# Causal attention's diagonal blocks packed into shared score columns, with zero-padded copies of V

## The chip, the cores and the metric

The kernel runs on one core of a Trainium2 chip. The metric is the device time of one execution in microseconds (us): the median of two runs is 317.3 (317.27 and 317.34). A core has five instruction queues that matter here: PE (TensorE, matrix products; its weight loads are listed apart as PEld), DVE (VectorE), ACT (ScalarE), POOL (GpSimd) and SP (SyncE), which here only issues DMAs. Each works through its own instructions in order and waits on the others by semaphores.

## The reference

2,048 tokens of width 640 go through a layer norm; an attention branch and a gated branch read the result, and the input is added at the end. The attention works on four segments of 512 tokens, with 32 heads of 20 columns. Inside a segment it is a causal softmax; a memory matrix per head carries the sums of the segments before.

```python
for s in range(N):                                   # N = 4 segments, L = 512
    logits = jnp.einsum('bhqd,bhkd->bhqk', qs, ks) * scale + mask
    p = _softmax(logits, axis=-1)
    a_dot = jnp.einsum('bhqk,bhkd->bhqd', p, vs)
    pq = phi(qs)
    num = jnp.einsum('bhld,bhde->bhle', pq, M)
    den = jnp.einsum('bhld,bhd->bhl', pq, z)[..., None] + 1e-06
    o = g * (num / den) + (1.0 - g) * a_dot
    M = M + jnp.einsum('bhld,bhle->bhde', phi(ks), vs)
    z = z + jnp.einsum('bhld->bhd', phi(ks))
...
g = _silu(_B_ref(xn, B_w_gate, B_w_up, B_w_down))    # (sigmoid(x Wg) * (x Wu)) Wd
return x + s * g
```

The mask lets query q see key k only if k <= q. Of the 512x512 scores of a head and segment, a little over half count.

## The kernel before, in words

**Layout.** Heads are worked on in 8 groups of four per segment. `KT` and `QT` hold keys and queries transposed: for group g, head r of the four has 20 rows from partition 32r on, and three more rows that carry a bound on the scores. So a score product has 23 rows, and the four heads of a group stand in four row strips of the PE array (`tile_position=(32 * r, 0)`). `V` holds values with tokens on partitions, 21 columns a head, the last of them ones, so that the sum of the weights comes out beside the weighted values; two such buffers alternate between segments.

**Score units.** `Sps` is one accumulator of 128x4x512: keys of one block of 128 on partitions, four heads, 512 columns of queries. A unit (`pair_units`, `scores`) fills it once, ACT turns it into weights with one exponential (`exps`, line 558) and POOL sets the weights above the diagonal to zero in each diagonal block of 128x128 (line 560). Key block 0 needs all 512 queries, block 1 the last 384, block 2 the last 256, block 3 the last 128. For two groups that makes five units: 512; 384+128; 256+256 of both groups; 512; 384+128. A segment has 20 units, and the kernel 80. There is one `Sps`, so the next unit's scores wait for the exponential of the last; up to four tiles of weights (`pt`) are kept.

**Values.** `attend_T` (a visit) computes weighted values for one group, transposed: four column strips of the PE array, one a head, 32 columns of V each (`tile_position=(0, 32 * r)`), four key blocks in turn into one accumulator `ApsT`. It comes two to four units after the group's scores. DVE turns the result (line 582), POOL scales it (590, 591), DVE turns it back (594). The last group of the last segment is done by `attend` instead, with the weights as the stationary side and results in token order.

**The order.** Everything is written out by hand order: one slot per score unit. At the start of a slot stands a visit, if one is due, then the unit's scores, and then other work up to the slot's share. The dense products (gate `gp`, up `up`, down `yp`) are cut into single matmuls and fill what is free; the rest (projections `psq`, `psv`, the memory products `am` and `dm`, output products `sp`, DMAs on SP's queue, DVE steps) has due times in slots in the table `TIMES`. In a slot ahead of a visit, dense matmuls are written as four quarter-width ones (`ORDER["columns"]`, line 128), otherwise as one (line 124).

**Shared buffers.** `mn` is a staging tile used by the phi step (`phi_min`) and by the first two normalised tiles of the next segment (`ln_norm`); the other two have tiles of their own. At the start of the kernel `mn` also holds the zeros for the first warming matmuls. `cb`, `dmb` and `o6` have tiles of their own. Normalised tiles are spilled to DRAM by SP (line 270) and come back transposed (274).

Of the kernel before, what the change touches and what calls it, by code (L numbers as in the profile page):

```python
# [9 lines left out]
P = 128  # L10
D = 640
H = 32
DH = 20
E1 = DH + 1
# [29 lines left out]
def pair_units(g):  # L44
    return [[(g, 0, 0, 512, 0)],
            [(g, 1, 0, 384, 128), (g, 3, 384, 128, 384)],
            [(g, 2, 0, 256, 256), (g + 1, 2, 256, 256, 256)],
            [(g + 1, 0, 0, 512, 0)],
            [(g + 1, 1, 0, 384, 128), (g + 1, 3, 384, 128, 384)]]

def segment_units(n):
    units = []
    for g in range(0, NG, 2):
        units += pair_units(g)
    return units

TIMES = dict(
    turn=(0.03, 0.27, 1.29), turn_last=(0.0, 0.135, 0.43), attend=0.36, last=(0.36, 0.75), rest=350, dot6=0.43, load6=0.48,
    dot7=1.92, load7=1.95, add=(4.27, 4.52), out=(5.25, 5.95, 7.25, 8.35, 8.74, 9.06, 9.45, 11.05), update=-1.2,
    mem=(2.23, 4.32, 3.0, 6.98, 6.98, 2.45, 9.09, 10.79), mem_spill=11.56, mem_T=14.4, mem_T_last=12.63,  # L60
    k_tok=2.04, dot3=13.22, dot5=17.84, load5=18.1, add5=19.86, dot6_last=19.55, load6_last=19.6, stats0=(0.53, 0.9, 1.65, 3.6),
    stats=(-0.55, 0.13, 1.32, 3.57), norm=(5.26, 5.72, 6.03, 6.29), norm_T=7.22, ready=12.0,
    K=(9.69, 10.07, 10.49, 13.82, 14.29), Q=(11.32, 11.72, 12.29, 12.45, 13.52), K_eng='vaava', Q_eng='avvav',
    V=(10.33, 13.33, 14.43, 14.63, 17.05, 17.66, 19.78, 20.06), V_eng='avaavvav', k_spill0=14.77, k_lay0=15.15,
    q_spill0=14.1, q_lay0=16.79, q_spill1=15.26, k_spill1=16.93, q_abs=(13.53, 14.84), bound=14.78,
    bound_mm=15.9, bound_lay0=18.6, load_x=13.95, phi_k=((7.15, 7.62, 8.3), (12.77, 13.52, 13.77)),
    phi_q=((16.0, 16.6, 17.12), (18.3, 18.7, 19.18)),
# [8 lines left out]
def kernel(  # L76
# [71 lines left out]
    warm = stg.tile([P, 3 * L], BF, name="mn")  # L148
    nc.vector.memset(warm[:, 0:L], 0.0)
# [33 lines left out]
    V = [t[:, 0:VN].rearrange("p (j h e) -> p j h e", j=4, e=E1) for t in Vflat]  # L183

# [7 lines left out]
    def late_constants(after):  # L192
# [7 lines left out]
        ones_columns(1)  # L200
        nc.gpsimd.memset(obs[0][:], 0.0)
# [39 lines left out]
    def ln_norm(n, j, mv, rs):  # L241
        if n > 0 and j < 2:
            if j == 0:
                seg["xn"] = stg.tile([P, 3 * L], BF, name="mn")
# [745 lines left out]
```

## Time and profile before

| | us | share of the span |
|---|---|---|
| median of two runs | 317.3 | |
| the profiled execution | 317.5 | |
| its span, first to last instruction | 315.7 | |
| granted clock over the span | 1.000 | |
| exponentials, 80 of 1.878 | 150.2 | 48% |
| masks, 128 of 0.660 | 82.5 | 26% |
| first score unit starts on PE | 35.9 | |
| last score unit starts on PE | 297.4 | |
| last matmul ends, about | 312.0 | |

A row of the groups view names the line, the engine, the operation, what it writes from what, the shapes and the count; behind the bar stand the busy time of the group, the mean duration of one instruction in ns, and the time that its engine sat idle ahead of it, with what ended most of it. In the timeline each row is a merged run of like instructions: its start, its length, and what it is. Lengths of matmuls include the way through the array and overlap with the next one's; what a run takes from PE is the distance from its start to the next run's start.

### The profile page before, as it was taken

What the parts mean: (1) busy time and instruction counts of PE and PEld (TensorE: products, weight loads), DVE (VectorE), ACT (ScalarE), POOL (GpSimd) and SP (SyncE); (2) the same over time, 40 slices, a digit from 0 to 9 for tenths busy, and PEclk for the clock granted to TensorE, in tenths of its full rate; (3) what the DMA queues carried; (4) which work ended last, traced back from release to release, by engine and by line L of the source; (5) the groups of instructions that cost most, each with busy time, mean ns of one, the idle gap of its engine ahead of it and who ended that gap; (6) DMA issues with size and microseconds to landing.
All of it is one profiled execution on the core that took longest, in us unless ns stands there. A gap on an engine that the chain in (4) does not pass through costs nothing.

```text
span 315.7 us, 10227 instructions
## 1 busy us (share of the span) xinstructions
PE 307.1 (97%) x4297; PEld 167.5 (53%) x4327; DVE 224.9 (71%) x507; ACT 226.6 (72%) x228; POOL 133.5 (42%) x231
## 2 busy tenths in 40 slices
PE   7999999999999999999999999999999999999995
PEld 4544444665545444654665454545466655444673
DVE  5473455654868988878869989788787776644575
ACT  3724478778798776778897869679897775777730
POOL 2870035535262544435453364444444353525313
PEclk9999999999999999999999999999999999999999
DMA  7984886410742383504953365239524000280202
GB/s 242 375 329 148 282 227 175 127 45 2 209 149 66 101 140 118 129 24 148 263 171 110 115 106 144 67 110 211 175 78 131 19 23 26 79 148 25 86 21 85
DMA packets 55246, 41.27 MB, mean 131 GB/s; under 512 B 25952, under 2 KB 53824, under 8 KB 55200
## 3 DMA queue, kind: packets, MB, share of 16 engines
q1 hardware_dynamic: 52656, 35.87, 41.4%
q10 hardware_dynamic: 2544, 4.75, 4.1%
q8 instruction: 34, 0.56, 0.7%
q14 instruction: 12, 0.10, 0.1%
HBM read 19.98 MB, written 14.73 MB: 110 GB/s over the span
## 4 chain that ended last, share of the span: by engine, by line
PE 95%; DMA 1%; issue 1%; DVE 1%; ACT 1%; SPq 0%; ACTq 0%
PE up L124 11%; PE gp L124 10%; PE yp L124 10%; PE psq L124 10%; PE Sps L550 8%; PE gp L128 6%; PE yp L128 6%; PE up L128 6%; PE ApsT L574 6%; PE psv L124 5%; PE psq L128 4%; PE sp L124 3%; PE sp L128 3%; PE psv L128 2%; PE sp L534 2%; DMA xt<-in_A_x_dram 1%
## 5 line engine op out<-in xcount | busy, mean ns | idle before, releaser
L558 ACT ACTIVATE pt<-Sps 128x2048 bf16<-128x2048 f32 x80 | 150.2, 1878 | 40.6 <-PE Sps L550 39.6
L560 POOL TENSOR_SCALAR_AFFINE_SELECT pt<-pt 128x512 bf16<-128x512 bf16 x128 | 82.5, 660 | 156.6 <-ACT pt L558 153.8
L437 DVE SCALAR_TENSOR_TENSOR hT<-tg,up 128x512 bf16<-128x512 bf16 x48 | 32.6, 678 | 24.0 <-PE up L124 10.0
L124 PE MATMUL up<-xnT,Wu 128*128 128x512 bf16 x146 | 40.3, 380 | 1.4 <-issue 1.1
L124 PE MATMUL gp<-xnT,Wg 128*128 128x512 bf16 x146 | 38.9, 379 | 0.6 <-issue 0.5
L426 ACT ACTIVATE tg<-gp 128x512 bf16<-128x512 f32 x48 | 28.6, 595 | 14.4 <-PE gp L124 10.0
L124 PE MATMUL yp<-Wd,hT 128*128 128x320 bf16 x246 | 38.2, 300 | 0.0
L550 PE MATMUL Sps<-QT,KT 23*128 23x384 bf16 (+3 forms) x512 | 31.9, 301 | 0.1
L124 PEld LDWEIGHTS <-hT 128*128 128x128 bf16 x246 | 22.7, 98 | 11.3 <-issue 3.0
L454 DVE SCALAR_TENSOR_TENSOR aa<-t,yp 128x320 bf16<-128x320 bf16 x32 | 15.3, 478 | 13.9 <-ACT t L453 13.8
L582 DVE STREAM_TRANSPOSE tb<-ApsT 128x512 f32<-128x512 f32 x31 | 22.0, 711 | 4.1 <-PE ApsT L574 4.0
L128 PE MATMUL gp<-xnT,Wg 128*32 128x512 bf16 x352 | 24.4, 380 | 0.0
L574 PE MATMUL ApsT<-pt,V 128*32 128x512 bf16 (+2 forms) x496 | 23.5, 299 | 0.0
L124 PEld LDWEIGHTS <-Wu 128*128 128x128 bf16 x159 | 14.2, 98 | 17.4 <-issue 4.0
L124 PEld LDWEIGHTS <-Wg 128*128 128x128 bf16 x152 | 14.1, 98 | 15.8 <-issue 1.9
L128 PE MATMUL yp<-Wd,hT 128*32 128x320 bf16 x552 | 21.9, 300 | 0.0
L128 PE MATMUL up<-xnT,Wu 128*32 128x512 bf16 x324 | 21.7, 380 | 0.0
L550 PEld LDWEIGHTS <-KT 23*128 23x128 bf16 x512 | 9.2, 92 | 23.5 <-issue 23.4
L594 DVE STREAM_TRANSPOSE obT<-ob 128x256 f32<-128x256 f32 x31 | 13.5, 434 | 11.1 <-POOL ob L591 11.0
L591 POOL TENSOR_TENSOR ob<-tb,rb 128x320 bf16<-128x320 f32 x27 | 19.9, 735 | 2.2
L124 PE MATMUL psq<-xnT,Wq 128*128 128x512 bf16 x82 | 19.4, 379 | 0.2
L124 PE MATMUL psv<-Wv,xnT 128*128 128x320 bf16 x115 | 18.5, 300 | 0.4 <-ACT xnT L670 0.4
(124 smaller groups left out, 442.2 us busy)
## 6 DMA issues: line engine op xcount, KB each, us to landing
KT<-Kd SPq DMA_DIRECT2D x32, 80.0 KB
QT<-Qd SPq DMA_DIRECT2D x32, 80.0 KB
out_dram<-xt SPq DMA_DIRECT2D x14, 160.0 KB
Wg<-in_B_w_gate_dram ACTq DMA_DIRECT2D x1, 1920.0 KB
Wu<-in_B_w_up_dram ACTq DMA_DIRECT2D x1, 1920.0 KB
xt<-in_A_x_dram SPq DMA_DIRECT2D x3, 640.0 KB
Wd<-in_B_w_down_dram SPq DMA_DIRECT2D x1, 1920.0 KB
Od<-odot SPq DMA_DIRECT2D x3, 640.0 KB
```

Source lines behind the costliest of these rows:

```text
L124: nc.tensor.matmul(out_, lhsT=lhsT, rhs=rhs, start=start, stop=stop, skip_group_check=True)
L128: nc.tensor.matmul(out_[cols], lhsT=lhsT[:, cols], rhs=rhs, start=start, stop=stop, tile_position=(0, 32 * r), skip_group_check=True)
L426: nc.scalar.activation(tg[:], gp[:], ACT.Tanh, scale=0.5)
L437: nc.vector.scalar_tensor_tensor(out=h[:], in0=seg[n]["tg"][:], scalar=1.0, in1=up[:], op0=ALU.add, op1=ALU.mult)
L454: nc.vector.scalar_tensor_tensor(out=s["aa"][j][:, hs], in0=t2[:], scalar=1.0, in1=yp[:], op0=ALU.add, op1=ALU.mult)
L550: nc.tensor.matmul(Sps[:, r, c0:c0 + ncol], lhsT=KT[32 * r:32 * r + DH + 3, g, kb * P:(kb + 1) * P], rhs=QT[32 * r:32 * r + DH + 3, g, q0: ...
L558: nc.scalar.activation(pt[:, :, 0:ntot], Sps[:, :, 0:ntot], ACT.Exp, scale=SCALE)
L560: nc.gpsimd.affine_select(out=pt[:, :, c0:c0 + P], in_=pt[:, :, c0:c0 + P], compare_op=ALU.is_ge, fill=0.0, base=0, pattern=[[0, 4], [1, P ...
L574: nc.tensor.matmul(ps[32 * r:32 * r + 32, q0:L], lhsT=Vflat[n % 2][:, off:off + 32], rhs=t[:, r, c0:c0 + ncol], start=(i == 0), stop=(i == ...
L582: nc.vector.transpose(tb[:].rearrange("p h e -> p (h e)"), ps[:].rearrange("p (a t b) -> p a b t", t=32, b=2))
L591: eng.tensor_tensor(to, of, by, op=ALU.mult)
L594: nc.vector.transpose(s["obT", g // 4][:, g % 4, :].bitcast(F32), ob[:].rearrange("p a e b -> p (a e b)").bitcast(F32))
```

## The change

The units are cut anew (`segment_units`). The 128 keys of a diagonal block are taken in halves of 64. Early queries of a block see only its first half of keys, and two such products, from two key blocks, are put one above the other in the same 64 score columns: one on partitions 0 to 63, one on 64 to 127. A unit is of one of three kinds, all 512 columns wide:

- A, one per group: keys 0-63 with all queries on the low half of the partitions; on the high half, keys 64-127 with queries from 64 on, and, in the first 64 columns, keys 128-191 with queries 128-191.
- B, one per group: keys 128-255 with queries from 192 on (320 columns) and keys 256-383 with queries from 320 on (192 columns), on all partitions.
- C, one per four groups: 128 columns a group. In the first 64, keys 256-319 with queries 256-319 on the low half and keys 384-447 with queries 384-447 on the high half; in the other 64, keys 384-447 and keys 448-511 with queries from 448 on.

That makes 8 + 8 + 2 = 18 units and slots a segment, 72 in all. Products onto one half of the partitions have 64 weight columns (tiles of 32x64), B's have 128. A column block that holds two key blocks is read twice by the value products, each time with a copy of V in which the partitions of the other are zero: `Z` holds, for one half of the groups, key blocks 0 and 2 on partitions 0-63 and key blocks 1 and 3 on 64-127, with zeros elsewhere. It is cleared once, and refilled by two DMAs on SP's queue for each half segment. A visit has 8 pieces instead of 4. Each mask becomes one for each pattern (152 in all for 128). The last `attend` takes queries in blocks of 64.

Buffers: three `pt` and one `ptc` for four `pt`; `mn` holds three normalised tiles, and the fourth shares a tile (tag `sc`) with `cb`, `dmb` and `o6`; `o6` is cleared in the last segment instead of at the start; the warming zeros lie in `ktok`'s tile. The due times in `TIMES` are rewritten for 18 slots, most of them as 0.9 of the old.

```diff
+HALF = P // 2
+GH = NG // 2
 def segment_units(n):
     units = []
-    for g in range(0, NG, 2):
-        units += pair_units(g)
+    for h in range(2):
+        for i in range(GH):
+            units += [("A", GH * h + i), ("B", GH * h + i)]
+            if i == 0:
+                units.append(("C", h))
     return units
...
+    ZW = H // 2 * E1
+    Zflat = cpool.tile([P, 4 * ZW + 32 - E1], BF, name="Z")
+    Z = Zflat[:, 0:4 * ZW].rearrange("p (a b w) -> p a b w", a=2, b=2)
+
+    def fill_Z(n, h):
+        src = Vflat[n % 2][0:HALF, 0:VN].rearrange("p (a b k w) -> p a b k w", a=2, b=2, k=2)
+        for b in range(2):
+            nc.sync.dma_start(Z[HALF * b:HALF * b + HALF, :, b, :], src[:, :, b, h, :])
...
+        nc.gpsimd.memset(Zflat[:], 0.0)
...
     def ln_norm(n, j, mv, rs):
-        if n > 0 and j < 2:
-            if j == 0:
-                seg["xn"] = stg.tile([P, 3 * L], BF, name="mn")
+        if j == 0:
+            seg["xn"] = stg.tile([P, 3 * D], BF, name="mn")
+        if j < 3:
             xn = seg["xn"][:, j * D:(j + 1) * D]
         else:
-            xn = lnp.tile([P, D], BF, name="xn", bufs=2)[:]
+            xn = stg.tile([P, D], BF, name="xn", tag="sc")[:]
...
+    def products(pieces):
+        for out_, keys, g, q0, q1 in pieces:
+            m, p0 = keys.stop - keys.start, out_[0]
+            for r in range(4):
+                rows = slice(32 * r, 32 * r + DH + 3)
+                nc.tensor.matmul(Sps[p0:p0 + m, r, out_[1]:out_[1] + q1 - q0], lhsT=KT[rows, g, keys],
+                                 rhs=QT[rows, g, q0:q1], start=True, stop=True, tile_position=(32 * r, p0))
+
     def scores(unit):
...
+        kind, g = unit
+        k = slice
+        if kind == "A":
+            products([((0, 0), k(0, 64), g, 0, L), ((HALF, 64), k(64, 128), g, 64, L),
+                      ((HALF, 0), k(128, 192), g, 128, 192)])
+        elif kind == "B":
+            products([((0, 0), k(128, 256), g, 192, L), ((0, 320), k(256, 384), g, 320, L)])
+        else:
+            for i in range(GH):
+                c, e = P * i, GH * g + i
+                products([((0, c), k(256, 320), e, 256, 320), ((HALF, c), k(384, 448), e, 384, 448),
+                          ((0, c + 64), k(384, 448), e, 448, L), ((HALF, c + 64), k(448, L), e, 448, L)])
 
     def exps(unit):
...
+        pt = ptp.tile([P, 4, L], BF, name="ptc" if kind == "C" else "pt", bufs=1 if kind == "C" else 3)
+        nc.scalar.activation(pt[:], Sps[:], ACT.Exp, scale=SCALE)
...
+        if kind == "A":
+            mask(low, lambda t: t[:, :, 0:64], [[0, 4], [1, 64]], 0)
+            mask(high, lambda t: t[:, :, 0:P].rearrange("p r (b c) -> p r b c", b=2), [[0, 4], [0, 2], [1, 64]], 0)
+        elif kind == "B":
+            for c0 in (0, 320):
+                mask(slice(0, P), lambda t: t[:, :, c0:c0 + 64], [[0, 4], [1, 64]], 64)
+        else:
+            mask(low, lambda t: t.rearrange("p r (i b c) -> p (r i) b c", b=2, c=64)[:, :, 0, :],
+                 [[0, 4 * GH], [1, 64]], 0)
+            for i in (0, GH // 2):
+                cols = slice(P * i, P * i + P * GH // 2)
+                mask(high, lambda t: t[:, :, cols].rearrange("p r (b c) -> p r b c", c=64),
+                     [[0, 4], [0, GH], [1, 64]], 0)
...
+    def pieces(n, g, which):
...
+        out = [(a, 0, 64, 64, L), (a, "Z0", 0, 0, 64), (a, "Z1", 0, 128, 192),
+               (b, 1, 0, 192, L), (b, 2, 320, 320, L),
+               (c, "Z2", i, 256, 320), (c, "Z3", i, 384, 448), (c, 3, i + 64, 448, L)]
...
-    def attend(n, todo):
+    def attend(n, which):
...
+        for values, v, t, c0, q0, q1 in pieces(n, NG - 1, which):
             for r in range(4):
...
+                for q in range(q0, q1, HALF):
+                    p0 = q % P
+                    nc.tensor.matmul(acc["ps"][p0:p0 + HALF, q // P, r, :],
+                                     lhsT=t[:, r, c0 + q - q0:c0 + q - q0 + HALF], rhs=src[:, off:off + E1],
+                                     start=p0 not in acc["begun"], stop=True, tile_position=(0, p0),
+                                     skip_group_check=True)
...
+    fill_Z(0, 0)
     load_x(1)
...
-    SLOTS, SEG = len(units), 20
+    SLOTS, SEG = len(units), 4 * GH + 2
...
+    for n in range(NSEG):
+        for g in range(NG if n < NSEG - 1 else NG - 1):
+            visits[unit_of[n, "B", g] + (3 if g % GH == 0 else 2)] = (n, g)
...
+        for h in range(2):
+            if n or h:
+                at(t0 + TIMES["fill"][h], 0, fill_Z, n, h)
```

## The prediction

> **What bounds the kernel now.** I read the engine totals and the slices of the page first, then the chain, then the costliest groups, and then single stretches of TensorE's timeline, because the totals leave only one engine to look at.
>
> ```profile
> PE 307.1 (97%) x4297; PEld 167.5 (53%) x4327; DVE 224.9 (71%) x507; ACT 226.6 (72%) x228; POOL 133.5 (42%) x231
> ...
> PE   7999999999999999999999999999999999999995
> ...
> PEclk9999999999999999999999999999999999999999
> ...
> PE 95%; DMA 1%; issue 1%; DVE 1%; ACT 1%; SPq 0%; ACTq 0%
> ...
> L558 ACT ACTIVATE pt<-Sps 128x2048 bf16<-128x2048 f32 x80 | 150.2, 1878 | 40.6 <-PE Sps L550 39.6
> L560 POOL TENSOR_SCALAR_AFFINE_SELECT pt<-pt 128x512 bf16<-128x512 bf16 x128 | 82.5, 660 | 156.6 <-ACT pt L558 153.8
> ```
>
> PE is busy in nine tenths or more of every slice but the first and the last, at a full granted clock, and is 95% of the chain. The exponentials wait for PE (39.6 us), not PE for them. So shorter ACT work moves nothing; the time changes by what changes on PE. Busy is not price, so I price PE by the distance from one start to the next:
>
> ```profile
> 45.70 0.59 PE L124 MATMUL gp<-xnT,Wg 128*128 128x512 bf16 x2
> 46.23 0.39 PE L550 MATMUL Sps<-QT,KT 23*128 23x512 bf16 x4
> 46.56 0.83 PE L128 MATMUL gp<-xnT,Wg 128*32 128x512 bf16 x12
> 47.21 1.25 PE L128 MATMUL up<-xnT,Wu 128*32 128x512 bf16 x20
> 48.29 1.25 PE L128 MATMUL gp<-xnT,Wg 128*32 128x512 bf16 x20
> 49.37 0.72 PE L574 MATMUL ApsT<-pt,V 128*32 128x512 bf16 x16
> 50.02 0.40 PE L550 MATMUL Sps<-QT,KT 23*128 23x384 bf16 x8
> 50.35 1.25 PE L124 MATMUL up<-xnT,Wu 128*128 128x512 bf16 x4
> ...
> 98.25 0.81 PE L390 MATMUL dm<-V,ktok 128*32 128x63 bf16 x80
> 98.87 0.41 PE L128 MATMUL gp<-xnT,Wg 128*32 128x512 bf16 x4
> ...
> 298.38 0.75 PE L610 MATMUL Aps<-V,pt 128*128 128x21 bf16 x24
> ...
> 298.99 3.15 PE L124 MATMUL yp<-Wd,hT 128*128 128x320 bf16 x22
> ```
>
> Four things are read here. Twenty quarter-width matmuls of 512 columns take 1.08 us (47.21 to 48.29): four column tiles run together, 216 ns for 512 columns, 0.42 ns a column. Four row tiles of a score unit also run together (46.23 to 46.56), but 0.33 us is 0.11 more than 0.216: that is the change of tile shape. The same extra stands ahead of it (0.53 for two matmuls of 216). Eighty matmuls of 63 columns take 0.62 us, 7.8 ns each: singly, a round of four starts 28 to 30 ns after the last for the first 28, and then the matmuls come 8.3 ns apart. Full-width matmuls of 21 columns come 25 ns apart (0.61 over 24).
>
> **The change, part by part.** All PE terms are in us for the whole kernel; the code gives the counts, these rows the prices.
>
> *Changes of tile shape.* In program order the kernel before alters the shape 163 times, the changed one 151 times: 16 fewer around 8 fewer score units, 4 more around the two last attends, now in 128x64 tiles. At 0.105 each: -1.26. The new shapes' own changes aren't in the trace; the four kinds that are lie between 0.10 and 0.11.
>
> *Score streams.* Before, each of 32 groups streams 512, 384, 128 and 256 columns on four row tiles: 216 + 173 + 53 + 109 = 551 ns start to start, 17.6 in all. Now a group has A: 512 columns on one column half, 448+64 on the other. If the halves run together as the row tiles and the column tiles do, A takes the 216 of its longer half plus some 15 for the staggered starts: 231. B: 320+192 by the row of 384+128 (173 for the first): 226. C, per four groups, is 64 matmuls of 64 columns over eight tiles. Its lower end is 8 rounds of 29 = 232 ns, its upper end 64 matmuls at 8 ns = 512 (also the 16 rounds that half overlap would make). The nearest row, the 80 short ones, starts 28 at the pace of the tiles and then goes by 8.3: 28 x 29/8 + 36 x 8.3 = 400, which I take. Sum: 32 x 0.457 + 8 x 0.40 = 17.8, so +0.2 (from -1.1 to +1.1).
>
> *Values.* 31 visits of 32 matmuls for 16, over the same 1,280 columns: five short rounds at 29 to 32 ns where 27 would be the share of the columns, and four more matmul rounds at 2 to 3 ns. +11 ns a visit, +0.35 (0 to +0.75).
>
> *Last attends.* 80 matmuls of 21 columns for 40. If the two halves overlap, 12.5 ns each, the price stays at 1.0; if not, 25 each, +1.0. I take 0, since column tiles overlap in every row that has them.
>
> *Wide or narrow dense matmuls.* More of them stand in slots before a visit, so 2,288 quarter-width ones instead of 1,888; at 1.08 for twenty against 1.08 to 1.09 for five: 0.
>
> *ACT, POOL, DVE.* Eight exponentials fewer: 8 x 1.878 = 15.0 off ACT, none of it on the path. POOL's 128 masks become 152 over as many elements; 128x128 takes 290 ns and 128x512 takes 660, so 0.96 ns an element, and the 20-row mask of Ind (160 elements, 475) adds about 8 ns a row. A has 0.41+0.69, B 2 x 0.41, C 3 x 1.25. That is some +7 on 133.5 of 315.7: nothing, as long as C is in time (a rival). The clearing of Z is about 1.25 (840 elements take 0.80) in POOL's idle time from 22.6 to 38.3. The clearing of o6 (0.55) moves from 1.7 to the last segment: nothing.
>
> *Z copies.* Sixteen issues of 0.4 on SP's queue. The first pair stands between QT's bounds (done 31.87) and x, Wd, the second spill, the token-order K and the second relayouts: 0.8 later each. Wd is first read at 54.03, after 20 us of cover; without cover, 0.8 once. Later pairs follow oT's load and hold up its last part and the token-order K by 0.8: in the trace the load is issued at 109.24, the next spill at 110.26, and the reader of Z comes four slots after 102.60, about 117. The waits on Z's last reader are for a visit that is already past. Cost 0.
>
> *xn in mn.* The third normalised tile now shares mn with the phi step, whose minimum waits for that tile's spill. In the trace the spills are issued from 124.63, the minimum starts at 127.50 and the transpose, which needs both spills landed, at 127.62. So DVE might wait 0 to 0.3, three times, with the queued evacuations and turns behind it; PE has four rotating accumulators ahead of it. I take 0, at most +0.9. At the start xn loses one wait of 0.5 on a transpose, on DVE alone: 0.
>
> Sum: -1.26 + 0.2 + 0.35 + 0 = -0.7. The profiled execution took 317.5 (its span 315.7 and 1.8 around it), which makes 316.8; the median of the two runs is 317.3, so I forecast **316.6**. With the lower ends: -1.26 - 1.1 = -2.4, 314.9. With the upper ends: -1.26 + 1.1 + 0.75 + 1.0 = +1.6, 318.9.
>
> **Rivals.** *The column halves do not overlap (slower).* No row has row tiles and column tiles at once. Then A streams 216 + 189 + 29 = 434 instead of 231, 32 x 0.203 = +6.5, and C takes 512 instead of 400, +0.9. Together 316.6 + 7.4 = **324.0**. It passes 2% (6.3 us) only if nearly all of the overlap, 7.0 of 7.4, is lost. For it: each direction alone leaves the other whole. Against: four column tiles read all 128 rows at once without loss (47.21), twice the streams that the halves need. Chance 0.12. The Trainium skill (TensorE: Matmul & The Clock Gate, "Measured speedup vs the span model") reports that row and column tiles compose, nine tiles at 6.32 times one; no run here shows it yet, and it speaks for the forecast.
>
> *Loading 64 columns of weights sets the pace.* The trace has loads of 128 columns at full width within 25 ns (298.38) and of 32 in quarter tiles within 29 ns. If a load in column tiles goes by its columns, 64 take 58: C becomes 8 x 58 = 464 (+0.5), and 40 units that open with such a load are 29 later each (+1.2): 316.6 + 1.7 = **318.3**. For it: PE changes shape first and loads then. Against: the extra after a change is the same 0.10 to 0.11 for 32 and 128 columns. Chance 0.12. The Trainium skill says that column tiling rules out fast weight loads (TensorEngine Tiling (Array Packing), "Feature Incompatibilities") and puts a load at the columns over 1.2 ns (TensorE: Matmul & The Clock Gate, "LDWEIGHTS"), 53 ns for 64; with that C would be 427 and the sum 0.2 higher, and our 25 ns for full-width pairs is a faster load than that rule's 107.
>
> *C's masks come late.* The visit is two slots after C, and 73 slots over some 266 us are 3.65 each: about 6.8 us from C's scores to the visit. Exponential and its wait 2.1, three masks 3.75: 5.85. It decides from 1.57 us a mask on, and each 0.1 above costs 8 x 0.3 = 2.4; at 1.86 it is over 2%, at a price by rows of 165 ns (660 over 4) it would be **342**. Against it: 20 rows cost 475 in all. Chance 0.04.
>
> *Over 2% faster* would need 6.3 off PE; all that eight score units cost is 8 x 0.43 = 3.4. Chance 0.02. That fewer units are not made is excluded: 72 exponentials stand in the changed program.
>
> **How the numbers follow.** The forecast has 0.70. The range takes its own ends and the second rival's (318.3, and 1.2 for its unknowns), 314.7 to 319.5, and leaves out the first and third rivals and the faster case, 0.18. A measurement of this kernel tells 2% from no change. Faster 0.02; slower the third rival and somewhat over half of the first, 0.11; same the rest, 0.87.
>
> **What would show it.** Right: A's second four matmuls start within 0.02 us of the first four and the next work 0.34 after A's start; C's next work 0.34 to 0.6 after its start; a visit 0.66; 72 exponentials, ACT near 212, PE still at 97%. Wrong: A at 0.54 (first rival), a C unit near 0.6 with wider gaps ahead of every 64-column load (second), PE idle ahead of the first visit of each half (third), or a new idle on PE behind a DVE wait for Xd.

## The result

The changed kernel took 328.34 us (median of 2 runs, 328.19 to 328.48) beside 317.3 for the kernel before: a ratio of 1.0348, interval 1.0303 to 1.0392. The prediction was 316.6, in a range of 314.7 to 319.5, and none of its rivals' times (324.0, 318.3, 342) is near. The profiled execution took 328.48, its span 326.8, so 11.1 of span have to be found. The page of the changed kernel, in the rows that were read before:

```profile
PE 311.0 (95%) x5743; PEld 180.5 (55%) x5776; DVE 230.3 (70%) x507; ACT 213.6 (65%) x220; POOL 146.4 (45%) x256
...
PE   6999999999999999999998998899999999999995
...
PEclk9999999999999999999999999999999999999999
...
PE 72%; DMA 7%; DVE 7%; ACT 5%; SPq 4%; issue 3%; POOL 2%; ACTq 0%; DVEq 0%
...
L624 ACT ACTIVATE pt<-Sps 128x2048 bf16<-128x2048 f32 x64 | 120.0, 1875 | 39.1 <-PE Sps L602 34.8
L627 POOL TENSOR_SCALAR_AFFINE_SELECT pt<-pt 128x256 bf16<-128x256 bf16 (+2 forms) x128 | 64.9, 518 | 138.4 <-ACT pt L624 132.8
...
L627 POOL TENSOR_SCALAR_AFFINE_SELECT ptc<-ptc 64x1024 bf16<-64x1024 bf16 x24 | 28.3, 1195 | 16.1 <-ACT ptc L624 15.5
```

ACT's total is as forecast (213.6 for 212), and so is each C mask (1.2); POOL has 13 more where some 7 were forecast. The clock is full. What changed is the chain: PE had 95% of it and now has 72%; DVE, ACT, DMA and SP's queue have come in. PE's slices show 8s in the second half, where there had been only 9s. PE's timeline tells whether its own work is as priced:

```profile
48.89 0.42 PE L602 MATMUL Sps<-QT,KT 23*64 23x512 bf16 x12
49.25 1.05 PE L166 MATMUL up<-xnT,Wu 128*32 128x512 bf16 x16
...
52.49 0.36 PE L673 MATMUL ApsT<-pt,V 128*32 128x448 bf16 x4
...
53.16 0.40 PE L602 MATMUL Sps<-QT,KT 23*128 23x320 bf16 x8
...
79.29 0.71 PE L602 MATMUL Sps<-QT,KT 23*64 23x64 bf16 x64
79.93 0.39 PE L162 MATMUL gp<-xnT,Wg 128*128 128x512 bf16 x1
...
308.17 0.58 PE L710 MATMUL Aps<-V,pt 128*64 128x21 bf16 x25
...
309.21 2.08 PE L162 MATMUL yp<-Wd,hT 128*128 128x320 bf16 x14
```

A lasts 0.36 from its start to the next work, a visit 0.67: both as forecast, so the column halves overlap (in the trace's single records the second half's four matmuls start 13 ns behind the first four). C lasts 0.64 in place of 0.505 (0.40 and the change of shape). The first of the last attends takes 1.04 for 48 matmuls of 21 columns: 19.5 ns each, not 12.5.

To split the 11.1, I priced every matmul of each program, in its order, by the prediction's distances from start to start, with C and the last attends at what they measured. The real distance from the first scores to the last matmul, less that sum, is time in which PE waited, with whatever the prices have wrong. Before: 275.8 measured, 275.1 priced, 0.7 of waits. Changed: 285.4 measured, 275.9 priced, **9.5 of waits**. So PE's work costs 0.8 more (it should have been 0.7 less), the waits 8.8 more, and the first scores start at 37.33 in place of 35.87, 1.5 more: together 11.1. The largest waits behind the first scores, from the view of waits, with their sum, how many, and the longest:

```profile
PE sp L166 <- ACT tg L473: 1.5, 1, 1.5
PE psv L162 <- DVE aa L501: 1.4, 1, 1.4
PE Sps L602 <- ACT pt L624: 1.4, 3, 0.6
```

They are short and far apart, some behind ACT's work and some behind DVE's. The first of them in the timeline of the changed kernel (engines mixed, in order of time):

```profile
200.77 0.92 DVE L412 TENSOR_SCALAR mn<-ktok 128x1280 bf16<-128x1280 bf16 x1
...
201.72 1.27 ACT L417 ACTIVATE mn<-mn 128x1280 bf16<-128x1280 bf16 x1 [2.43 <-DVE mn L412]
...
202.90 1.86 ACT L624 ACTIVATE pt<-Sps 128x2048 bf16<-128x2048 f32 x1
...
203.14 0.61 PE L166 MATMUL gp<-xnT,Wg 128*32 128x512 bf16 x8
...
204.65 0.59 ACT L473 ACTIVATE tg<-gp 128x512 bf16<-128x512 f32 x1
...
205.29 0.46 PE L166 MATMUL sp<-Wo,oT 128*32 128x320 bf16 x8 [1.55 <-ACT tg L473]
```

ACT does its work in program order. Phi's exponential (L417) stands ahead of the exponential of the scores and waits 2.43 for its minimum, which DVE reaches only after the memory parts. The scores' exponential and the tanh of the gate behind it are late by as much, the gate's accumulator is not free, and PE waits 1.55 for one. In the kernel before, phi's exponential was due at 7.62, behind slot 7's exponential. Most due times from slot 2 on were scaled by 18 to 16 slots (2 + 5.62 x 8/9), not plainly by 0.9, which makes 6.996 of it: just ahead of slot 7's.

That gave theory O: the waits come from which steps share a slot and in which order they queue, since scaled due times fall otherwise on the grid of 18 slots. (The first four expectations still word it more narrowly, as slots with too little work between two score units.) Its first rivals were S (the staging buffers that are now shared) and Q (the Z copies on SP's queue).

### The profile page after: what moved, and what is told of

The parts are those of the page before. It is cut to its first block, busy times and chain, and to the rows that moved or that the text cites. A ratio compares the mean times of both kernels' runs of the same rounds, so it can differ in the third digit from the quotient of the medians.

```text
span 326.8 us, 13190 instructions
## 1 busy us (share of the span) xinstructions
PE 311.0 (95%) x5743; PEld 180.5 (55%) x5776; DVE 230.3 (70%) x507; ACT 213.6 (65%) x220; POOL 146.4 (45%) x256
## 4 chain that ended last, share of the span: by engine, by line
PE 72%; DMA 7%; DVE 7%; ACT 5%; SPq 4%; issue 3%; POOL 2%; ACTq 0%; DVEq 0%
PE psq L162 8%; PE up L162 7%; PE gp L162 7%; PE gp L166 7%; PE Sps L602 7%; PE up L166 6%; PE yp L162 6%; PE psq L166 4%; ACT pt L624 4%; PE ApsT L673 4%; PE yp L166 4%; PE psv L162 4%; PE sp L162 2%; SPq L514 2%; DMA xnT<-Xd 2%
## 5 line engine op out<-in xcount | busy, mean ns | idle before, releaser
L624 ACT ACTIVATE pt<-Sps 128x2048 bf16<-128x2048 f32 x64 | 120.0, 1875 | 39.1 <-PE Sps L602 34.8
L627 POOL TENSOR_SCALAR_AFFINE_SELECT pt<-pt 128x256 bf16<-128x256 bf16 (+2 forms) x128 | 64.9, 518 | 138.4 <-ACT pt L624 132.8
L627 POOL TENSOR_SCALAR_AFFINE_SELECT ptc<-ptc 64x1024 bf16<-64x1024 bf16 x24 | 28.3, 1195 | 16.1 <-ACT ptc L624 15.5
L602 PE MATMUL Sps<-QT,KT 23*64 23x64 bf16 (+4 forms) x1152 | 31.9, 257 | 1.4 <-ACT pt L624 1.4
L162 PE MATMUL yp<-Wd,hT 128*128 128x320 bf16 x197 | 30.9, 300 | 0.0
L166 PE MATMUL up<-xnT,Wu 128*32 128x512 bf16 x424 | 29.3, 380 | 0.0
L166 PEld LDWEIGHTS <-hT 128*32 128x32 bf16 x748 | 19.5, 97 | 7.0 <-issue 1.8
L602 PEld LDWEIGHTS <-KT 23*64 23x64 bf16 (+1 forms) x1152 | 13.8, 100 | 17.1 <-issue 14.4
L673 PE MATMUL ApsT<-pt,V 128*32 128x448 bf16 (+2 forms) x372 | 20.8, 300 | 0.4 <-DVE aa L545 0.4
L500 ACT ACTIVATE t<-yp 128x320 bf16<-128x320 f32 x32 | 13.8, 434 | 9.9 <-PE yp L162 6.8
```

Source lines behind the costliest of these rows:

```text
L162: nc.tensor.matmul(out_, lhsT=lhsT, rhs=rhs, start=start, stop=stop, skip_group_check=True)
L166: nc.tensor.matmul(out_[cols], lhsT=lhsT[:, cols], rhs=rhs, start=start, stop=stop, tile_position=(0, 32 * r), skip_group_check=True)
L500: nc.scalar.activation(t2[:], yp[:], ACT.Tanh, scale=0.25)
L602: nc.tensor.matmul(Sps[p0:p0 + m, r, out_[1]:out_[1] + q1 - q0], lhsT=KT[rows, g, keys], rhs=QT[rows, g, q0:q1], start=True, stop=True, ti ...
L624: nc.scalar.activation(pt[:], Sps[:], ACT.Exp, scale=SCALE)
L627: nc.gpsimd.affine_select(out=blocks(pt[rows]), in_=blocks(pt[rows]), compare_op=ALU.is_ge, fill=0.0, base=base, pattern=pattern, channel_ ...
```

## The experiments

"Waits" is worked out as above, on the profiled execution (the 8.5 of the expectations counts only those over 0.15 us). The ratios are those on record, which need not be the quotient of two medians. Times are in us.

| kernel | median (range, runs) | ratio to before, interval | waits |
|---|---|---|---|
| before | 317.3 to 317.8 by batch | | 0.7 |
| changed | 328.34 (328.2 to 328.5, 2) | 1.0348, 1.0303 to 1.0392 | 9.5 |
| a_own | 329.16 (327.9 to 331.5, 4) | 1.0374, 1.0322 to 1.0427 | 10.0 |
| a_nofill | 328.61 (328.2 to 329.7, 4) | 1.0354, 1.0330 to 1.0378 | 9.5 |
| b_share | 317.37 (317.1 to 318.1, 10) | 0.9998, 0.9988 to 1.0007 | |
| b_fill | 317.73 (317.2 to 318.2, 10) | 0.9999, 0.9985 to 1.0013 | |
| r_k | 331.59 (328.5 to 332.7, 4) | 1.0416, 1.0359 to 1.0472 | 12.4 |
| r_phi | 327.65 (327.0 to 328.4, 4) | 1.0308, 1.0279 to 1.0337 | 8.7 |
| b_k | 320.30 (319.3 to 322.0, 6) | 1.0088, 1.0059 to 1.0116 | 2.7 |
| b_phi | 324.26 (323.0 to 324.9, 4) | 1.0196, 1.0164 to 1.0227 | 5.8 |
| r_slots | 325.92 (324.6 to 327.1, 4) | 1.0266, 1.0224 to 1.0308 | 6.5 |
| c_wide | 328.95 (1) | | 13.4 |
| r_mix | 325.49 (324.5 to 326.1, 4) | 1.0241, 1.0217 to 1.0266 | 6.9 |
| r_mix_st | 325.00 (324.4 to 326.5, 4) | 1.0243, 1.0209 to 1.0278 | 7.0 |
| r_20 | 324.11 (321.7 to 326.5, 4) | 1.0198, 1.0125 to 1.0270 | 3.2 |
| b_early | 320.99 (320.7 to 321.3, 4) | 1.0099, 1.0081 to 1.0117 | 4.6 |
| b_late | 330.39 (330.2 to 331.3, 4) | 1.0405, 1.0380 to 1.0430 | 12.4 |
| r_20_cw | 320.50 (320.0 to 324.0, 5) | 1.0086, 1.0070 to 1.0103 | 7.9 |
| r_20_st | 323.10 (321.5 to 324.2, 4) | 1.0171, 1.0136 to 1.0206 | 4.6 |
| r_20_z | 323.17 (322.0 to 325.5, 6) | 1.0174, 1.0136 to 1.0212 | 4.0 |

### Is it the shared buffers or the Z copies?

a_own gives the third normalised tile a buffer of its own again; a_nofill leaves out all Z copies but the first pair, so later segments use the first one's values there. b_share puts the changed kernel's shared staging into the kernel before; b_fill adds 16 copies of V to the kernel before, on SP's queue at the same places (to a scratch tensor).

```
a_own     seg["xn"] = stg.tile([P, 3 * L], ...); j == 2: xn = stg.tile([P, D], BF, name="xn2")
a_nofill  for h in range(2): at(t0 + TIMES["fill"][h], ...)   removed
b_share   xn: mn (j < 3) or tag "sc"; cb, dmb: tag "sc"; mn = [P, 3 * D]; warm in ktok
b_fill    at(t0 + (1.5, 11.6)[h], 0, fill_Z, n, h)            added
```

> The changed kernel with a tile of its own for the third normalised tile; mn is as small as before. Theory S (shared staging): the phi step's minimum waits for the third tile's spill, ACT's queue stands behind its exponential, and PE runs into full accumulators; in the changed trace the stalls of PE at 130 to 135 and 199 to 205 us (about 3.5 us) are of this kind, so 324 to 326. Theory Q (Z copies make SP's queue late) and theory O (fewer, longer slots leave too little work between two score units): no change, 328.3.

> The changed kernel with only the first pair of Z copies; the 14 later DMAs are left out, so later segments read old copies of V. Theory Q: the Q spill and the second half of the phi step on Q come 1 to 3 us sooner, the stalls at 156 and 173 us (about 1.9) go, 325.5 to 326.5. Theories S and O: 328.3, at most 0.5 less.

> The kernel before with the changed kernel's staging buffers alone: three normalised tiles in mn, the fourth in one tile with cb, dmb and o6, the warming zeros in ktok's tile. Theory S: 3 to 5 us slower, 320 to 322. Theories Q and O: 317.3, within 0.5.

> The kernel before with the changed kernel's 16 copies of V on SP's queue at the same due times by its longer segment, into a scratch in DRAM that nothing reads. Theory Q: 1.5 to 3 us slower, 319 to 320. Theories S and O: 317.3, within 0.5.

Neither. Each taken away leaves the changed kernel where it was, and the largest wait, 1.55 for the gate's tanh, stays (at 205.29 in the changed kernel, 204.71 in a_own, 205.40 in a_nofill). Each added to the kernel before costs nothing, to within 0.15%. S and Q fall; the prediction's zeros for them stand.

### Single due times, in both kernels

r_k and r_phi undo one move each in the changed kernel; b_k and b_phi make the same two moves in the kernel before.

```
r_k    K[4]     12.924 -> 13.02
r_phi  phi_k[0] (6.578, 6.996, 7.6) -> (6.578, 7.3, 7.8)
b_k    K[4]     14.29 -> 13.95
b_phi  phi_k[0] (7.15, 7.62, 8.3) -> (6.578, 6.996, 7.6); mem[3], mem[4] 6.98 -> 6.427; out[2] 7.25 -> 6.667
```

> The changed kernel with one due time altered: the fifth K item of a segment moves from slot 12 (12.924) to slot 13 (13.02), as it stood before the change, where the fourth and the fifth K fell in two slots. Theory O (the due times, scaled by 0.9, fall otherwise on the grid of 18 slots, and PE waits where a slot is too short or a queue is in the wrong order): slots 13 and 49, which held two V pieces alone (1.8 us of PE work against an exponential of 1.88 and its hand-overs), grow to 2.9; the waits of PE at 90.7 and 229.0 us (0.66 each) and at 165.1 (0.22) go, 1.5 us in all, so 326.8 (325.5 to 327.3, more if the 1.5 us at 173 goes with them). Theory P (PE's own work is dearer than priced, the waits are only where slack shows): the same 328.3. Theory M (the waits move on to the next slot, since DVE and ACT are behind in any order): 327.9 to 328.6, with new waits of the same sum within three slots.

> The changed kernel with two due times altered: the exponential of the first phi step on ktok moves from 6.996 to 7.3, its end from 7.6 to 7.8, so that ACT does it after slot 7's exponential, as before the change, and not ahead of it. Theory O: ACT no longer stands 2.4 us at phi's minimum ahead of the exponential of the scores, the waits at 199.4 and 205.3 us (0.71 and 1.72) and at 130 to 135 (1.1) shrink to under 0.5 in all: 325.3 (324.8 to 326.5). Theory P: 328.3. Theory M: the minimum is as late as before and the wait shows up behind the next ACT or DVE work: 327.5 to 328.6.

> The kernel before, with the fifth K item moved from slot 14 (14.29) into slot 13 (13.95): slot 13 then holds two K, one Q and one V item (4.9 us of PE work), and slot 14 two V pieces alone (1.8), in each of the three segments, the pattern of the changed kernel. PE's work is the same. Theory O: one to three waits of 0.2 to 0.7 behind the short slots, as in the changed kernel: 318.6 (317.9 to 319.5). Theories P and M: within 0.4 of 317.4.

> The kernel before, with the last memory parts of the first half, the first phi step on ktok and the third output item given the slot times of the changed kernel (6.427, 6.427; 6.578, 6.996, 7.6; 6.667): phi's exponential then stands ahead of slot 7's on ACT. PE's work is the same. Theory O: ACT waits for phi's minimum ahead of the exponential of the scores, once in each of the segments 1 and 2, and PE waits 1 to 2.4 us each time: 320.3 (318.9 to 322). Theories P and M: within 0.5 of 317.4.

The kernel before answers as theory O says, and more strongly: b_k costs 2.5 and b_phi 6.5, both beyond the ranges expected. b_k, in its timeline, where the slot was left with two V pieces:

```profile
85.03 0.40 PE L550 MATMUL Sps<-QT,KT 23*128 23x384 bf16 x8
...
85.36 1.53 PE L124 MATMUL psv<-Wv,xnT 128*128 128x320 bf16 x10
85.54 1.88 ACT L558 ACTIVATE pt<-Sps 128x2048 bf16<-128x2048 f32 x1 [0.35 <-PE Sps L550]
...
87.47 0.40 PE L550 MATMUL Sps<-QT,KT 23*128 23x512 bf16 x4 [0.58 <-ACT pt L558]
```

PE has 1.8 us of work between two score units, the exponential between them ends 2.4 after the first unit's start, and the one score tile is not free: 0.64 lost, at 87.5, 154.5 and 220.6, once in each of the first three segments. b_phi, in the same view:

```profile
197.22 1.27 ACT L370 ACTIVATE mn<-mn 128x1280 bf16<-128x1280 bf16 x1 [2.10 <-DVE mn L365]
...
198.40 1.86 ACT L558 ACTIVATE pt<-Sps 128x2048 bf16<-128x2048 f32 x1
...
200.31 0.40 PE L550 MATMUL Sps<-QT,KT 23*128 23x512 bf16 x4 [2.12 <-ACT pt L558]
```

This is the start of the changed kernel's chain, phi's exponential ahead of that of the scores, made in the kernel before by due times alone. In the changed kernel the other way is only half open. r_phi takes the wait of 1.55 and the 0.45 at 135 away and gives 0.7 (forecast: 3). r_k takes away the waits behind two of the three short slots, as expected (0.26 stays at 167.2), but others stand where none or smaller ones had: 0.65, 0.97 and 0.43 at the bound's matmuls, which now come behind a longer slot. It is slower by 3.3 in the median, above the range of every theory (its profiled execution also starts at half clock, see the end). So r_phi lands in theory M's range, that a wait removed comes back elsewhere; in r_k more came back than went.

### A whole timetable on 18 slots, and C by itself

r_slots moves the steps of the kernel before by whole slots instead of scaling them. r_mix goes back to the scaled times and changes eight groups, each against a wait seen so far; r_mix_st also normalises the first tile ahead of the second tile's statistics. c_wide alters C alone.

```
r_slots  slots 2, 3 -> 2 and 18, 19 -> 17; slots 4 to 17 -> one lower
r_mix    add=(3.6, 3.8), out[2]=6.9, mem[3:5]=(5.98, 6.3), norm=(4.6, 4.95, 5.2, 5.45), norm_T=6.2,
         phi_k[0]=(6.62, 7.3, 7.8), K[4]=13.02, q_spill1=13.0, bound_mm=14.9
r_mix_st root0(0); norm0(0); half_stats0(1, 0); half_stats0(1, 1)
c_wide   products([((0, c), k(256, 320), e, 256, 384), ((HALF, c), k(384, 448), e, 384, L)])
```

> The changed kernel with the due times of its steps taken from the kernel before in another way: not multiplied by 0.9 but moved by whole slots, so that each step keeps its neighbours of before in its slot. Slots 2 and 3 of before become one, so do 18 and 19; slots 4 to 17 keep their contents and are numbered one lower. The work of PE is the same. Of the waits of PE over 0.15 us, 8.5 us in the changed kernel, theory O (they come from which steps share a slot) leaves under 3: 322.5 (320.5 to 325). Theory P (PE's own work is dearer than priced; retiming only moves what shows): 327 to 329. Theory M (18 slots hold the same DVE and ACT work per us whatever the grouping, and the waits come back elsewhere in the same sum): 327 to 329 with new waits of 6 us or more. Both kernels of this pair showed one half each: where the fifth K alone was moved, the waits came back at the bound's matmuls, and where phi's exponential alone was moved, 1.4 us went.

> The changed kernel with the packed unit C made of 32 matmuls of 128 columns in place of 64 of 64: the first two of each group's four pieces are widened over the other two's columns, so half of the packed products are other ones and the early queries' output is not the reference's. Columns streamed and everything behind it stay. C now takes 0.64 us from its start to the next work. If the number of matmuls sets its pace (8.3 ns a pair of load and matmul), the stream falls from 534 to about 270 ns: 0.37 to 0.40 us a unit, and PE's work is 2.1 us less in all. If the columns set it (eight tiles, four rounds of 56), it would have been 235 before as well, and the unit stays at 0.6 or more for another reason, such as a load of 64 columns of weights (53 to 58 ns a round: 0.34 to 0.37 here, 0.57 in the changed kernel): then a single pair's distance is not 8.3 but bunched by rounds of eight. The time: 326.2 by the first, 328.3 by the second, give or take 1.

> The changed kernel with eight groups of due times altered, each aimed at a wait of PE that its trace or those of the four retimed kernels show: the fifth K item back in its own slot (90.7, 165.1, 229.0 us) with the bound's matmuls half a slot later (the 2.0 that this had cost there); phi's first exponential after slot 7's (130 to 135, 205); the two memory parts ahead of it 0.45 and 0.13 slots apart from it (199); the sum of the outputs 0.4 slots earlier (261, 262); the second half of Q spilled ahead of the transposing load that holds SP's queue for 6 us (173); the normalised tiles and their transpose 0.3 to 0.4 slots earlier (69). Theory O (which steps share a slot, and the order in the queues, make the waits; 8.5 us in the changed kernel, 6 in the best retimed one): under 2.5 us of waits are left, 321.5 (319.5 to 324). Theory M (the waits come back elsewhere in the same sum): 325.5 to 329. By neither does it come under 318: C's 2.4 us and the last attends' 0.7 stay.

> The kernel with the eight altered groups, and at the start of the program the normalising of the first tile moved ahead of the statistics of the second: on DVE it then no longer stands behind a wait for the second tile of x, which lands at 4.9 us here and at 4.2 in the kernel before. If that wait is what makes PE idle 0.9 to 1.6 us ahead of the first transpose, the transpose starts at 5.3 to 5.5 in place of 6.0 to 6.4, the first scores 0.5 to 1.4 earlier, and the time is 0.5 to 1.4 below the same kernel without it. If the weights or later tiles set the start, nothing changes (within 0.3).

Regrouping is worth 2.4 to 3.3, and 6.5 to 7 of waits remain: r_slots meets neither theory's number, r_mix lands at the lower edge of theory M's. In r_slots none of the larger old waits is left, and new ones stand where slots were merged (1.2 at 172, where phi's exponential, the memory update and a score unit now meet). In r_mix a visit waits 1.1 for POOL's masks at 92.6, and an output item 1.1 for the gate's tanh at 258. By hand, no timetable for 18 slots was found that is free of waits. r_mix_st is level with r_mix, though the first transpose starts 0.2 earlier (5.39 against 5.56): that wait was not on the path.

c_wide tells what is dear in C:

```profile
43.74 0.43 PE L602 MATMUL Sps<-QT,KT 23*64 23x128 bf16 x32
44.10 1.04 PE L162 MATMUL gp<-xnT,Wg 128*128 128x512 bf16 x4
```

Half as many matmuls over the same columns: 0.36 in place of 0.64. Where the time goes is seen from the score matmuls in flight in the changed kernel's C at 79.29 (us, busy time, and their number in brackets):

```profile
79.28:79.44 0.16, 0.15 (x32) 0.00 (x0) 1.00 0.00 0
79.44:79.53 0.09, 0.09 (x33) 0.00 (x0) 1.00 0.19 52
```

Thirty-two start within the first 0.16 us; the 33 of the next row are these, still in flight, and one more. In the single records of the trace all eight C are alike: 32 matmuls in four bursts of eight, 139 ns in all; a pause of 100 ns; and the other 32 one by one, 8.3 ns apart (259 ns). c_wide's 32 come in four bursts alone, 80, 56 and 56 ns apart, the last two near the 54 that 128 columns take at 0.42 ns a column; they have neither the pause nor the single pace. So it is the second 32 that are dear. Why the pace changes behind the first 32 no run shows. The Trainium skill (TensorE: Matmul & The Clock Gate, "Measured speedup vs the span model") counts about 4 ns for each further tile of a pack; as an estimate, 64 at that would be 256 ns, and the stream takes 534. The first 32 agree, at 4.3 ns each; the others do not. And yet the time did not fall, in the one execution that there is: 2.2 of work left PE, and 3.9 of waits came, with another phase of everything behind it.

### The grid itself

r_20 runs the packed work, unchanged, on 20 slots a segment: two slots have no score unit, the visits stand at the slots of the kernel before, and the due times are those of the kernel before. b_early and b_late move the due times of the kernel before by a quarter of a slot, those tied to the visits excepted.

```
r_20     segment_units: after B of groups 1 and 5 a slot without a unit; SEG = 4 * GH + 4
         TIMES of the kernel before; zero=6.5, fill=(1.35, 11.6)
b_early  every due time from add on, turns and dot/load steps excepted: -0.25
b_late   the same: +0.25
```

> The changed kernel with a segment of 20 slots again, two of them without a score unit (after B of groups 1 and 5), so that the visits stand at slots 4, 6, 9, 11, 14, 16, 19, 21 as in the kernel before, and with the due times of the kernel before in place of the scaled ones. The packed units, the Z copies, the shared staging and the work of PE are those of the changed kernel: its PE work by the price of starts is 272.7 us behind the first scores, with C's 2.4 and the last attends' 0.8 on top 275.9, against 275.8 in the kernel before. Theory G (the grid: due times that no longer meet the slots make the waits): under 2.5 us of waits are left of 8.5, 319.0 (317.5 to 321). Theory W (the packed work itself makes the waits: visits of 32 matmuls that need Z and C's masks, and eight exponentials fewer that spaced the rest): 325 to 329, as on 18 slots.

> The kernel before with every due time but those tied to the visits (the turns, the spills and loads of the attention's output, the last attends) a quarter of a slot earlier, about 0.8 us. PE's work is the same, and no slot is left with less than 2.3 us of it. Theory G, in its strong form (the kernel before owes its 0.7 us of waits to due times that meet its slots, and any other phase costs several us, packed or not): 321 (319 to 324). Its weak form (only an overfull slot or a step that changes places with an exponential costs): 317.5 to 319. Theory W: within 0.7 of 317.5.

> The kernel before with the same due times a quarter of a slot later. Here the fifth K item and three others come to stand in one slot, and slot 35 is left with 1.1 us of PE work, slot 15 with 2.1. Theory G, strong: 322 (319.5 to 325). Weak: 318.5 to 320.5, from the short slots alone (0.6 each, and more at slot 35). Theory W: within 0.7 of 317.5.

The largest waits of b_late, which does the work of the kernel before:

```profile
PE Sps L587 <- ACT pt L595: 2.3, 3, 1.3
PE ApsT L611 <- DVE aa L491: 1.7, 1, 1.7
PE sp L165 <- ACT tg L463: 1.3, 1, 1.3
PE up L165 <- DVE aa L491: 1.2, 1, 1.2
```

and all of r_20's:

```profile
PE wps L741 <- DVE ktok L187: 1.2, 1, 1.2
PE pT L765 <- DVE mn L295: 0.6, 1, 0.6
PE cps L381 <- DVE ik L372: 0.4, 1, 0.4
PE psv L162 <- ACT xnT L770: 0.2, 1, 0.2
PE up L166 <- DVE hT L484: 0.2, 1, 0.2
```

A quarter slot later, about 0.8 us, costs the kernel before 12.8 us, more than the whole change did (theory G, strong, and beyond its range): 11.7 of waits, and 1.2 of work, since the moved steps also make 12 more changes of tile shape (175 for 163). A quarter slot earlier costs 3.4. With the old grid and its due times the packed kernel loses most of its waits: 9.5 go to 3.2. Of what the view lists all but 0.6 lies before the first scores; the rest of the 3.2 is in pieces too small for the view, or an error of the pricing. But of r_20's four times none lies in the range of theory G (317.5 to 321): 321.7 (the profiled one) and 322.3 are just above it, and 325.9 and 326.5 lie in theory W's. The lower two ran at a mean clock of 1.000, like both executions of the changed kernel (328.2 and 328.5). Among these the timetable made 6.3 of the 11; by the medians it made 4.2. So the timetable is a large part of the loss, over half at full clock, and not all of it.

### What is left on 20 slots

```
r_20_cw  C as in c_wide
r_20_st  bound_mm 15.9 -> 16.3; the first tile normalised ahead of the second tile's statistics
r_20_z   fill[0] 1.35 -> 1.02; dot6 0.43 -> 1.1, dot7 1.92 -> 1.85, load6 0.48 -> 1.9
```

> The packed kernel on 20 slots with C's 64 matmuls of 64 columns made 32 of 128, as before on 18 slots: half of the packed products are other ones, and the early queries' output is not the reference's. On 18 slots this took 0.28 us off each C and nothing off the time, since waits of as much stood elsewhere. If the waits are gone on 20 slots, PE's work shows in the time: 2.2 below the same kernel with C as it was, 319.5 in its undisturbed runs (321.7 to 322.3 were the lower two of that kernel's four), and C at 0.36. If the packing loses time in another way that fills whatever is freed, 321.5 to 326.

> The packed kernel on 20 slots with the bound's matmuls 0.4 slots later (16.3 for 15.9; they waited 0.6 us for DVE at 156.7) and the first tile's normalising ahead of the second tile's statistics at the start (0.6 us of idle PE ahead of the first transpose in that trace). By the sum: 321.7 less 0.6 and up to 0.4, 320.7 to 321.5 in undisturbed runs. If neither wait was on the path: 321.7 to 322.3. The four times of the kernel without these edits fell into 321.7 to 322.3 and 325.9 to 326.5; if the upper pair belongs to the kernel and not to those runs, it comes again here.

> The packed kernel on 20 slots, with the first pair of Z copies of each segment ahead of the spills of the attention's output and of the load that waits for them (1.02 in place of 1.35; the spills and loads behind it, at 1.1, 1.85 and 1.9). If the copies' landing is what the first visit of a segment waits for in the slower executions, no time lies above 323, the median is 321.0 (320.3 to 322.3) in place of 324.1, and the trace shows no wait of a visit for Z. If the spread has another cause, the times lie between 321.5 and 326.5 again. By neither does it pass the kernel before (317.5): C's 2.4, the last attends' 0.8 and some 1.5 of other waits stay.

On this grid C's saving shows: four of r_20_cw's five times are 320.0 to 321.5. Its profiled execution is the fifth, 324.0, and shows what made it so:

```profile
176.19 2.60 SPq L519 DMA_DIRECT2D OTd<-obT  x4
...
180.38 0.38 SPq L526 DMA_DIRECT2D oT<-OTd  x1
...
180.87 1.70 SPq L229 DMA_DIRECT2D Z<-V  x2
...
183.36 0.36 PE L672 MATMUL ApsT<-pt,V 128*32 128x448 bf16 x4
...
184.94 0.21 PE L672 MATMUL ApsT<-pt,Z 128*32 128x64 bf16 x4 [1.22 <-DMA Z<-V]
...
186.32 0.24 PE L672 MATMUL ApsT<-pt,Z 128*32 128x64 bf16 x4 [1.16 <-DMA Z<-V]
```

The load of oT waits on SP's queue for the spill ahead of it to land; the Z copies stand behind it, are issued at 180.87 and land after the visit has begun. r_20_st's profiled execution has the same wait at 185 to 187 and gains nothing. r_20_z moves these copies ahead of the load: its profile has no wait for Z, but its times still lie between 322.0 and 325.5. So the copies explain a part of the two longer profiles, and not the spread. The granted clock goes with the spread: of the ten kernels in the table that have an execution with a mean clock of 0.995 or less, it is the longest one in nine (r_20's two long times stand at 0.995, its two short ones at 1.000). r_20_cw's profile, at 0.995, shows what such a mean can hold. Right behind its two waits the clock's row, the third number from the end, is near a half:

```profile
186.00:188.00 2.00, 1.68 (x33) 0.83 (x34) 0.80 (x2) 0.20 (x1) 0.00 (x0) 0.59 0.23 63
188.00:190.00 2.00, 2.00 (x9) 1.01 (x8) 1.68 (x5) 1.81 (x2) 0.25 (x1) 0.56 0.96 123
```

By these rows (0.41 + 0.44) x 2 = 1.7 us of full clock are lost on top of the waits' 2.4. What decides which execution gets such a stretch stays open. No kernel with all of the packed work came below 321.5, and without any wait r_20 would be at 318.4: 276.7 of priced work (0.8 more than on 18 slots, for 8 more changes of shape), 35.9 ahead of the first scores, 4.0 behind the last matmul's start, 1.8 around the span.

## Why the prediction was wrong

Right, by its own steps: the changes of shape (0.10 to 0.115 with the new shapes too), A and B, the visits, the masks in time (1.2 against the 1.57 that would decide), the full clock, the Z copies and the shared staging at 0 in this kernel (a_own, a_nofill, b_share, b_fill). The first rival is refuted by A's 0.36. The second, 58 ns for a load of 64 columns, is not seen: the extra after a change is the same for 64 columns, and in C's first bursts, which come 32 ns apart after the first, each tile takes such a load. (c_wide could not tell, since it halves the loads too.)

**The failed step** is the sentence "So shorter ACT work moves nothing; the time changes by what changes on PE". It read the kernel before as a PE with slack around it. The slack was there, but whether PE waits was decided by the timetable: b_late does the same work in the same kernel and has 11.7 more of waits. The change rewrote the whole timetable, and the sum had no term for that: phi's exponential crossed slot 7's, the fifth K moved into its neighbour's slot (6.5 and 2.5 us when the kernel before makes these moves alone), and 8.8 of the 11.1 are waits of PE. Which move made which of them is shown for a few only. No rival held them either. The nearest sentence, that DVE might wait at mn "0 to 0.3, three times", looked at one buffer. The rows for it were at hand: due time by due time, which steps share a slot before and after, and what stands on each queue beside them.

**Sizes.** C was taken at 400 ns and measured 534, above the forecast's upper end of 512: 8 x 0.134 = 1.1 more. Its picture, quick rounds first and 8.3 ns each afterwards, was right; the pause of 100 ns between them was missing, and that 64 at 8.3 ns also make 531 is chance. The last attends were taken at 0 and cost 0.6 (19.5 ns in place of 12.5 for each of 80; 0.8 with the changes of shape behind them, which the sum had counted), inside the bound of 1.0. Together they turn PE's own gain of 0.7 into a loss, so the packing had nothing to give even without a wait. The start, 1.5 later, was not in the sum. The first transpose comes at 6.00 in place of 5.32, behind the second tile of x, and from there the psv matmuls start 267 ns apart until 10.25, where those of the kernel before are 136 apart from 6.79 on. That this makes the 1.5 is argued: in the four profiles of packed kernels with such a stretch (the changed one, a_nofill, r_k, r_phi) the first scores start at 36.9 to 37.7, in the others at 35.9 to 36.9.

**Not settled:** whether 18 slots allow a timetable without waits (besides the changed kernel's five were tried, 6.5 to 12.4 left); what decides the spread of the packed kernels on 20 slots; and why the second tile of x lands later in most packed programs (DVE, in the order that both kernels have, takes it up at 4.47 to 5.46 in them, at 4.13 to 4.28 in those of before), though nothing that loads it was changed.

## What to carry to other kernels

Where one engine is busy 95% of the time and others 70%, the spare time of the others is a property of the order written down, not of their totals: a change of the grid that the order hangs on is a change of its own, to be made and measured alone, by moving the old kernel's steps by a quarter slot, for instance. When steps are re-timed, list for each slot what it holds, and for each in-order queue who stands ahead of whom, before and after; a slot with less PE work than one exponential, and an exponential that passes another, could each be read from the due times. And count small matmuls by number as well as by columns: here the second half of 64 cost nearly twice what the first did, the pause between them apart.

## What the runs showed of the hardware

Beside the two paces of C (32 matmuls of 64 columns in 139 ns, the next 32 in 259 behind a pause of 100): the matmuls behind a short idle can run at half pace. r_k's first transpose comes after 1.63 us of idle; its windows (us, busy time of the engines, then the granted clock as the third number from the end):

```profile
7.00:9.00 2.00, 1.76 (x12) 1.10 (x12) 1.93 (x8) 0.93 (x3) 0.08 (x1) 0.71 1.07 386
9.00:11.00 2.00, 2.00 (x9) 1.15 (x8) 1.40 (x5) 1.12 (x2) 1.55 (x4) 0.50 1.07 364
```

In the changed kernel, after 0.94 us of idle, the first five psv matmuls take 1.51 us where the kernel before takes 0.97, though its clock row reads 1.00 there; the first transposes run at half pace in both (107 ns apart; 56 later). It does not always happen: in r_20_z, after 1.50 us, the five take 0.85. The Trainium skill (TensorE: Matmul & The Clock Gate, "What's actually happening") has the half rate come after an idle window of about 3.4 us. The half rate agrees with the row of 0.50; in r_k under 2 us of idle came before it, 5 us into the program, and in r_20_cw (0.59 and 0.56 above) two waits of 1.22 and 1.16 us with four matmuls between them.
